# Attention projections of a float32 kernel: two 64-row products per tile, each in its own half of the array, in place of one 128-row product with block-diagonal weights

## The chip, the core and the metric

The kernel runs on one core of one Trainium2 chip. Its engines are TensorE (PE in the profile; its weight loads are listed apart as PEld), VectorE (DVE), ScalarE (ACT) and GpSimd (POOL); SyncE (SP) starts most of the DMA transfers. The metric is the device time of one execution in microseconds, as the median of several.

## The reference

All inputs are float32. Three stages follow each other. The change concerns the first line of the first one.

```python
def phi(x):                                  # q, k: [4, 8, 576, 64]; w_phi: [64, 128]
    proj = np.einsum('bhsd,df->bhsf', x, w_phi)
    proj = proj - np.max(np.abs(proj), axis=-1, keepdims=True)
    return np.concatenate([np.exp(proj), np.exp(-proj)], axis=-1)
q_p, k_p = phi(q), phi(k)
kv = np.einsum('bhsf,bhsd->bhfd', k_p, v)
z = np.sum(k_p, axis=2)
out = np.einsum('bhsf,bhfd->bhsd', q_p, kv) / (np.einsum('bhsf,bhf->bhs', q_p, z)[..., None] + 1e-06)
...
g = elu(x @ w_in)                            # x: [2304, 512], w_in: [512, 2048]
x = g @ w_out
...
out += p[:, e:e + 1] * (relu(x @ w1[e]) @ w2[e])      # 4 experts
```

## The kernel before, in words

The attention is done for 16 pairs of heads (4 batches, 4 pairs each). `pair(i)` (line 180) is a generator; it holds the work of one pair, and a new pair is started every five steps. The keys and the queries of a pair lie transposed in one tile `kq`: the 64 features of the first head on partitions 0 to 63, those of the second on 64 to 127. There is one `kq` buffer, loaded by two DMA transfers (lines 145 and 148).

**The projection** (`proj`, line 196). The weights `wbd` are block-diagonal: 128 rows by 2 times 128 columns, with `w_phi` for the first head in the upper left and for the second in the lower right. A product of one 128-token tile of `kq` (the stationary operand, 128 rows by 128 columns) with `wbd` (the moving operand, 256 columns) gives the features of both heads at once; half of what it multiplies is zeros. `proj` is called twice for the keys and twice for the queries, and each call fills one PSUM bank with two token tiles.

- In the first seven pairs (`wide`, `NF32 = 7`) this is a plain float32 matmul (line 203). The profile shows a float32 matmul as two PE records.
- In the other nine pairs `halves` (line 187) first splits the source in a high part `sh` (ACT, line 192) and a low part `sl` (POOL, line 193), both of type float32r, and a tile takes three float32r matmuls (lines 205, 206, 207), one PE record each.

The last 64 tokens of the keys and queries go through one matmul of their own in every pair (line 225, plain float32, block-diagonal).

**Behind the projection** `guard` (lines 213 and 214, DVE) takes the maximum of each row's absolute values and subtracts it; `kexp` (lines 217 and 218, ACT) makes the two exponentials of the keys; line 253 transposes the queries on PE, lines 266 and 271 take their exponentials; lines 246 and 247 multiply keys and values into `pk`, which line 295 copies to `kvw` or `kvh`; line 326 multiplies this with the queries' exponentials; line 328 copies the result to `nd`; its denominators go through DRAM (`den`, `dn`, `rec`, `rb`) and line 350 divides.

**What runs beside it.** DVE, ACT and POOL also convert the weights of the second stage from the start on (lines 111 to 128), and from about 88 us on PE computes the second stage (`Elu`, lines 512 to 514 and 541 to 543) between the pieces of attention. The third and largest part (lines 632 to 634, 711 to 713 and 734 to 736) comes behind the attention. All PSUM banks of the first two stages come from one pool of seven (line 87).

The order of each engine's instructions is made by a scheduler when the program is built (`schedule_with_timeline_sim=True`, line 982), so a change in one line moves others. Every engine then works through its list in order.

## Time and profile before

| | |
|---|---|
| median of 3 runs | 1417.33 us (1415.44 to 1420.01) |
| span of the profiled execution | 1417.7 us |
| PE busy | 1370.6 us, 97% of the span, 8040 records |
| DVE, ACT, POOL busy | 696.4 us, 640.9 us, 441.9 us |
| granted TensorE clock, mean of the span | 0.99 of full speed |

The profile page gives no time of the execution beside the span; the span lies 0.4 us above the median of the runs. PE's busy time counts the modelled duration of each matmul, with its way out of the array, so that neighbours overlap: of two matmuls in a row the start-to-start distance is what the stream costs. The granted clock is PE's clock as a share of its full speed.

### The profile page before, as it was taken

How to read it: one execution, taken by the hardware profiler on the slowest of the kernel's cores; microseconds unless marked ns; L12 is line 12 of the kernel's file. 1: busy time of each engine (PE TensorE's matmuls, PEld its weight loads, DVE VectorE, ACT ScalarE, POOL GpSimd, SP SyncE). 2: the span in 40 equal slices, each digit the busy share in tenths (PEclk: the TensorE clock that was granted, in tenths of full speed). 3: DMA queues.
4: the chain of work that ended last, by engine and by line, in shares of the span. 5: the costliest groups of instructions: out<-in, count | busy, mean ns of one | idle time of the engine just before them, and what ended most of it. 6: DMA issues, size and time to landing. Idle time of an engine off the chain costs nothing.

```text
span 1417.7 us, 21567 instructions
## 1 busy us (share of the span) xinstructions
PE 1370.6 (97%) x8040; PEld 1268.7 (89%) x8040; DVE 696.4 (49%) x1233; ACT 640.9 (45%) x1436; POOL 441.9 (31%) x506
## 2 busy tenths in 40 slices
PE   7899889999899899999999999999999999999998
PEld 6789889999899899999898989888888989889897
DVE  7878778654264576685434423224432325323332
ACT  6777777675455656574333442122431214321121
POOL 5667778552235211263202340002420004300000
PEclk9999999999999999999999999999999999999999
DMA  5554555321324230446334133434145351433422
GB/s 166 159 157 131 155 160 165 94 85 48 102 64 123 60 107 28 134 167 207 135 112 190 52 124 122 156 112 148 52 142 205 99 187 45 141 114 131 176 70 68
DMA packets 105593, 173.51 MB, mean 122 GB/s; under 512 B 33264, under 2 KB 50800, under 8 KB 105488
## 3 DMA queue, kind: packets, MB, share of 16 engines
q1 hardware_dynamic: 100592, 162.70, 35.6%
q10 hardware_dynamic: 4896, 9.44, 1.8%
q8 instruction: 63, 1.03, 0.3%
q14 instruction: 42, 0.34, 0.1%
HBM read 118.21 MB, written 53.89 MB: 121 GB/s over the span
## 4 chain that ended last, share of the span: by engine, by line
PE 71%; DMA 5%; DVE 4%; issue 2%; ACT 2%; POOL 1%; SPq 0%; DVEq 0%; ACTq 0%; POOLq 0%
PE bank L634 9%; PE bank L632 9%; PE bank L633 9%; PE bank L734 9%; PE bank L735 9%; PE bank L736 9%; PE bank L711 2%; PE bank L712 2%; PE bank L713 2%; PE bank L542 1%; PE bank L326 1%; PE bank L543 1%; PE bank L541 1%; PE bank L512 1%; PE bank L514 1%
## 5 line engine op out<-in xcount | busy, mean ns | idle before, releaser
L633 PE MATMUL bank<-xv,w 128*128 128x384 f32 x840 | 282.5, 336 | 0.0
L632 PE MATMUL bank<-xv,w 128*128 128x384 f32 x840 | 279.3, 337 | 3.0 <-DVE c L683 2.3
L634 PE MATMUL bank<-xv,w 128*128 128x384 f32 x840 | 278.4, 336 | 0.0
L734 PE MATMUL bank<-w,h 128*128 128x512 f32 x576 | 226.0, 395 | 2.1 <-ACT h L648 2.1
L735 PE MATMUL bank<-w,h 128*128 128x512 f32 x576 | 227.6, 395 | 0.0
L736 PE MATMUL bank<-w,h 128*128 128x512 f32 x576 | 202.9, 396 | 0.0
L474 POOL TENSOR_TENSOR w<-wst,w 128x256 fp32r<-128x256 f32 x100 | 78.0, 800 | 363.0 <-ACT w L473 347.8
L632 PEld LDWEIGHTS bank<-xv,w 128*128 128x128 f32 x840 | 158.0, 188 | 11.6 <-DVE c L683 2.6
L633 PEld LDWEIGHTS bank<-xv,w 128*128 128x128 f32 x840 | 158.1, 188 | 4.7
L634 PEld LDWEIGHTS bank<-xv,w 128*128 128x128 f32 x840 | 157.7, 188 | 0.0
L649 DVE SCALAR_TENSOR_TENSOR h<-bank,h 128x384 fp32r<-128x384 f32 x144 | 77.2, 554 | 126.1 <-ACT h L648 126.0
L648 ACT ACTIVATE h<-bank 128x384 fp32r<-128x384 f32 x144 | 66.7, 489 | 151.2 <-PE bank L634 94.8
L734 PEld LDWEIGHTS bank<-w,h 128*128 128x128 f32 x576 | 108.3, 188 | 25.0 <-ACT h L648 3.1
L735 PEld LDWEIGHTS bank<-w,h 128*128 128x128 f32 x576 | 108.4, 188 | 22.9
L736 PEld LDWEIGHTS bank<-w,h 128*128 128x128 f32 x576 | 107.3, 188 | 21.7 <-DVE h L649 1.0
L638 ACT ACTIVATE cmab<-bank 128x384 f32<-128x384 f32 x60 | 29.4, 491 | 191.8 <-PE bank L634 191.8
L583 POOL TENSOR_TENSOR xv<-xs,xv 128x768 fp32r<-128x768 f32 x24 | 46.8, 1954 | 192.3 <-ACT xv L582 183.7
L542 PE MATMUL bank<-gl,w 128*128 128x256 f32 x288 | 81.7, 287 | 4.3 <-DVE gl L525 3.7
L646 DVE TENSOR_TENSOR c<-cmab,bank 128x384 f32<-128x384 f32 x48 | 26.6, 554 | 117.4 <-ACT cmab L638 117.4
L512 PE MATMUL bank<-xh,w 128*128 128x256 f32 x288 | 84.1, 292 | 0.0
L646 DVE TENSOR_TENSOR bank<-cm,bank 128x384 f32<-128x384 f32 x48 | 26.9, 561 | 114.4 <-PE bank L634 100.7
L513 PE MATMUL bank<-xl,w 128*128 128x256 f32 x288 | 81.8, 284 | 0.0
(127 smaller groups left out, 2948.8 us busy)
## 6 DMA issues: line engine op xcount, KB each, us to landing
xv<-xvd SPq DMA_DIRECT2D x42, 768.0 KB
wst<-in_w SPq DMA_DIRECT2D x64, 256.0 KB
xvd<-xv SPq DMA_DIRECT2D x21, 768.0 KB
yscr<-y SPq DMA_DIRECT2D x54, 256.0 KB
y<-yscr SPq DMA_DIRECT2D x54, 256.0 KB
w<-in_w_in SPq DMA_DIRECT2D x32, 256.0 KB
w<-in_w_out SPq DMA_DIRECT2D x32, 256.0 KB
kq<-in_kq SPq DMA_DIRECT2D x16, 320.0 KB
```

Of the source, the lines that this page charges most:

```text
L474: on[WL[v % len(WL)]].tensor_tensor(out=lo, in0=x, in1=f32(hi), op=ALU.subtract)
L512: PE.matmul(ph[:, j], w[:, 0, c], xh[:, kc], start=(kc == 0), stop=False)
L513: PE.matmul(ph[:, j], w[:, 0, c], xl[:, kc], start=False, stop=False)
L542: PE.matmul(o, w[:, 0, c], self.gl[:, j], start=False, stop=False)
L632: PE.matmul(o, hi[:, c], x[:, 0, kc], start=not more and kc == 0, stop=False, skip_group_check=more)
L633: PE.matmul(o, hi[:, c], x[:, 1, kc], start=False, stop=False, skip_group_check=more)
L634: PE.matmul(o, lo[:, c], x[:, 0, kc], start=False, stop=kc == 1, skip_group_check=more)
L648: A.activation(h[:, 0], c, ACTF.Relu)
L649: V.scalar_tensor_tensor(out=h[:, 1], in0=c, scalar=0.0, in1=f32(h[:, 0]), op0=ALU.max, op1=ALU.subtract)
L734: PE.matmul(self.acc, h[:, 0, c], w[:, 0], start=f == 0, stop=False)
L735: PE.matmul(self.acc, h[:, 0, c], w[:, 1], start=False, stop=False)
L736: PE.matmul(self.acc, h[:, 1, c], w[:, 0], start=False, stop=f == 2 * NQ - 1)
```

## The change

`proj` now takes a whole source (keys or queries, 512 tokens) and returns two banks, one for each head. For each of the four token tiles it issues two plain float32 matmuls, one for each head: the stationary operand is 64 rows of `kq` (partitions 0 to 63 or 64 to 127) by 128 columns, the moving operand 64 rows of `wbd` by 128 columns. This holds for all 16 pairs: `halves`, `sh`, `sl`, `wbh` and `wbl` are gone. `guard` of a bank now works on one head and four tiles, not on two heads and two tiles; `kv` and `tpose` index accordingly. The matmul of the last 64 tokens (line 225, now 205) stays as it was. In the changed file, lines below the change have numbers lower by 19.

```diff
-    wbh = a1.tile([P, 2, FEAT], F32R, name="wbh")
-    wbl = a1.tile([P, 2, FEAT], F32R, name="wbl")
...
-    A.activation(wbh, wbd, ACTF.Copy)
-    G.tensor_tensor(out=wbl, in0=wbd, in1=f32(wbh), op=ALU.subtract)
...
-        def halves(src):
-            if wide:
-                return src, None
-            sh = a1.tile([P, 512], F32R, tag="sh", name="sh")
-            sl = a1.tile([P, 512], F32R, tag="sl", name="sl")
-            A.activation(sh, src, ACTF.Copy)
-            G.tensor_tensor(out=sl, in0=src, in1=f32(sh), op=ALU.subtract)
-            return sh, sl
-
-        def proj(halves, j):
-            sh, sl = halves
-            ps = bank()
-            for t in range(2):
-                c = slice((2 * j + t) * P, (2 * j + t + 1) * P)
-                o = ps[:, t * 256:(t + 1) * 256]
-                if wide:
-                    PE.matmul(o, sh[:, c], wbd, start=True, stop=True)
-                    continue
-                PE.matmul(o, sh[:, c], wbh, start=True, stop=False)
-                PE.matmul(o, sl[:, c], wbh, start=False, stop=False)
-                PE.matmul(o, sh[:, c], wbl, start=False, stop=True)
+        def proj(src):
+            ps = [bank() for _ in range(2)]
+            for t in range(4):
+                for h in range(2):
+                    r = slice(h * D, h * D + D)
+                    PE.matmul(blocks(ps[h], 4)[:, t], src[r, t * P:(t + 1) * P], wbd[r, h], start=True, stop=True)
             return ps
...
-        kh = halves(kt)
...
-        guard(kp[0][:, :, 1], proj(kh, 0), 4)
+        pk0, pk1 = proj(kt)
+        guard(kp[0][:, :, 1], pk0, 4)
...
-        guard(kp[1][:, :, 1], proj(kh, 1), 4)
-        qh = halves(qt)
+        guard(kp[1][:, :, 1], pk1, 4)
...
-        guard(qd[0], proj(qh, 0), 4)
+        pq0, pq1 = proj(qt)
+        guard(qd[0], pq0, 4)
...
-        guard(qd[1], proj(qh, 1), 4)
+        guard(qd[1], pq1, 4)
...
-                PE.matmul(pk[:, 2 * h + c], kp[t // 2][:, t % 2 * 2 + h, c], v[:, 4 * h + t], start=(t == 0), stop=False)
+                PE.matmul(pk[:, 2 * h + c], kp[h][:, t, c], v[:, 4 * h + t], start=(t == 0), stop=False)
...
-                    PE.transpose(blocks(pt, 4)[:, 2 * h + t], qd[j][:, 2 * t + h], ident)
+                    PE.transpose(blocks(pt, 4)[:, 2 * h + t], qd[h][:, 2 * j + t], ident)
```

What the scheduler makes of it is shown at three places. The first is PE's list at a wide pair: the keys' projection, the products of line 326 of the pair ahead, the queries' projection, the queries' transposes. Before:

```order
L203 MATMUL bank<-wbd,kq 128x256 x4
L326 MATMUL bank<-ew,kvw 128x288 x4
L203 MATMUL bank<-wbd,kq 128x256 x2
L326 MATMUL bank<-ew,kvw 128x288 x4
L203 MATMUL bank<-wbd,kq 128x256 x2
L253 MATMUL bank<-ident,qd_479 128x128 x4
L246 MATMUL bank<-vt_202,kp_476 128x128 x2
L246 MATMUL bank<-vt_202,kp_477 128x128 x2
```

And now, at the same pair:

```order
L188 MATMUL bank<-wbd,kq 128x128 x8
L307 MATMUL bank<-ew,kvw 128x288 x4
L188 MATMUL bank<-wbd,kq 128x128 x8
L307 MATMUL bank<-ew,kvw 128x288 x4
L234 MATMUL bank<-ident,qd_491 128x128
L227 MATMUL bank<-vt_200,kp_488 128x128 x4
```

All eight products of the queries now stand ahead of the second half of line 326 (now 307), where two of four stood; and the first transposes no longer stand together, since each group of four needs both `qd` tiles.

The second place is PE's list at pair 7, the first that was split: its keys' projection, with the semaphores it waits for. Before:

```order
L205 MATMUL bank<-wbh,sh 128x256 [waits PE_49,Activation_49]
L206 MATMUL bank<-wbh,sl 128x256 [waits Pool_49]
L207 MATMUL bank<-wbl,sh 128x256
L205 MATMUL bank<-wbh,sh 128x256
L206 MATMUL bank<-wbh,sl 128x256
L207 MATMUL bank<-wbl,sh 128x256
L541 MATMUL bank<-gh,w 128x256
```

These are the first two of the four token tiles. Now all four stand together; the same pair's keys, and a piece of the second stage ahead and behind:

```order
L494 MATMUL bank<-xl,w 128x256
L495 MATMUL bank<-xh,w 128x256
L188 MATMUL bank<-wbd,kq 128x128 [waits PE_49,Activation_49] x2
L188 MATMUL bank<-wbd,kq 128x128 x6
L522 MATMUL bank<-gh,w 128x256
```

Six products of 256 columns for two tiles have become four of 128, and the wait for POOL is gone; the first product of each head now waits for a bank of its own.

The third place is POOL's list around two split sources (`gl` belongs to the second stage, `w` and `top` to the conversion of its weights). Before:

```order
L525 TENSOR_TENSOR gl<-g,gh 128x512 [waits PE_49,Activation_49]
L193 TENSOR_TENSOR sl<-kq,sh 128x512 [waits DMAHW6_49,Activation_49]
L119 TENSOR_TENSOR w_1862<-w_1862 128x256 [waits DMAHW4_49,DVE_49]
L121 TENSOR_TENSOR top<-top,w_1862 128x256 [waits DMAHW2_49,Pool_49]
L119 TENSOR_TENSOR w_1936<-w_1936 128x256 [waits DMAHW6_49,DVE_49]
L121 TENSOR_TENSOR top<-top,w_1936 128x256 [waits DMAHW3_49,Pool_49]
L525 TENSOR_TENSOR gl<-g,gh 128x512 [waits Activation_49]
L119 TENSOR_TENSOR w_2058<-w_2058 128x256 [waits DMAHW0_49,DVE_49]
L193 TENSOR_TENSOR sl<-kq,sh 128x512 [waits DMAHW5_49,Activation_49]
```

And now:

```order
L506 TENSOR_TENSOR gl<-g,gh 128x512 [waits PE_49,Activation_49]
L119 TENSOR_TENSOR w_1902<-w_1902 128x256 [waits DMAHW1_49,DVE_49]
L121 TENSOR_TENSOR top<-top,w_1902 128x256 [waits DMAHW0_49,Pool_49]
L119 TENSOR_TENSOR w_1979<-w_1979 128x256 [waits DMAHW6_49,DVE_49]
L121 TENSOR_TENSOR top<-top,w_1979 128x256 [waits DMAHW3_49,Pool_49]
L506 TENSOR_TENSOR gl<-g,gh 128x512 [waits Activation_49]
L119 TENSOR_TENSOR w_2090<-w_2090 128x256 [waits DMAHW0_49,DVE_49]
```

The two subtractions of line 193, each behind an ACT result, have left the list; the rest keeps its order. From the attention's last product of line 326 to the end (5500 instructions of PE), the list of PE is the same in both programs.

## Rows read from the trace of the kernel before

**Rows 1.** Four stretches: length, PE, PEld, DVE, ACT, POOL busy (records), PEclk, DMA, GB/s.

```profile
0.00:88.00 88.00, 73.43 (x433) 63.21 (x434) 68.51 (x156) 62.33 (x163) 52.44 (x82) 1.00 0.55 163
88.00:200.00 112.00, 100.73 (x752) 95.44 (x751) 87.02 (x182) 80.59 (x199) 83.53 (x107) 0.97 0.51 151
200.00:369.00 169.00, 166.63 (x1374) 164.22 (x1373) 102.68 (x183) 114.33 (x268) 97.74 (x111) 1.00 0.32 96
369.00:1417.70 1048.70, 1029.82 (x5487) 945.85 (x5485) 438.23 (x714) 383.67 (x807) 208.22 (x207) 1.00 0.36 120
```

**Rows 2.** Timeline of PE, a wide pair: start us, us, instructions, idle before.

```profile
21.18 2.10 PE L326 MATMUL bank<-ew,kvw 128*128 128x288 f32 x8
23.12 1.03 PE L203 MATMUL bank<-wbd,kq 128*128 128x256 f32 x4
23.98 2.10 PE L326 MATMUL bank<-ew,kvw 128*128 128x288 f32 x8
...
27.22 1.06 PE L246 MATMUL bank<-vt,kp 128*128 128x128 f32 x8
28.12 0.39 PE L247 MATMUL bank<-vt,kpm 128*128 128x128 f32 x2
...
36.70 2.21 PE L326 MATMUL bank<-ew,kvw 128*128 128x288 f32 x8 [2.02 <-ACT kvw L295]
...
43.78 0.63 PE L253 MATMUL bank<-ident,qd 128*128 128x128 f32 x4 [1.20 <-DVE qd L214]
```

**Rows 3.** Timeline of PE, two token tiles of a split pair.

```profile
213.39 0.28 PE L205 MATMUL bank<-wbh,sh 128*128 128x256 f32 x1
...
213.98 0.28 PE L207 MATMUL bank<-wbl,sh 128*128 128x256 f32 x1
214.10 0.28 PE L512 MATMUL bank<-xh,w 128*128 128x256 f32 x1
```

**Rows 4.** Line 246 alone: ns min/median/max, first and last start us.

```profile
L246 PEld LDWEIGHTS bank<-vt,kp x512: 189/192/193, 13.8 to 361.2; 128*128 128x128 f32 x171
L246 PE MATMUL bank<-vt,kp x512: 272/276/276, 13.9 to 361.3; 128*128 128x128 f32 x171
```

**Rows 5.** Groups of instructions, 0 to 520 us: busy us, mean ns, idle before.

```profile
L213 DVE TENSOR_REDUCE mx<-bank 128x4 f32<-128x512 f32 x64 | 43.7, 686 | 16.0 <-PE bank L207 13.9 <-PE bank L203 1.7
...
L203 PE MATMUL bank<-wbd,kq 128*128 128x256 f32 x112 | 29.2, 398 | 1.0 <-DVE md L214 1.0
...
L193 POOL TENSOR_TENSOR sl<-kq,sh 128x512 fp32r<-128x512 f32 x18 | 23.4, 1300 | 27.5 <-ACT sh L192 24.6 <-issue 2.2 <-POOL xl L313 0.7
...
L214 DVE TENSOR_TENSOR kp<-bank,mx 128x512 f32<-128x512 f32 x32 | 21.9, 684 | 0.3
...
L205 PE MATMUL bank<-wbh,sh 128*128 128x256 f32 x72 | 21.5, 298 | 4.8 <-DVE g L523 1.7 <-ACT ew L266 1.6 <-ACT sh L192 1.4
...
L192 ACT ACTIVATE sh<-kq 128x512 fp32r<-128x512 f32 x18 | 11.3, 627 | 7.0 <-PE bank L207 5.3 <-issue 1.6
```

**Rows 6.** Line 203 from 88 us on, line 205 from 200 us on, alone.

```profile
L203 PE MATMUL bank<-wbd,kq x20: 378/380/484, 89.3 to 119.9; 128*128 128x256 f32 x20
L205 PE MATMUL bank<-wbh,sh x51: 275/280/393, 202.0 to 351.4; 128*128 128x256 f32 x51
```

**Rows 7.** Timeline of PE, 160 to 200 us: the longest idle times.

```profile
165.25 0.39 PE L205 MATMUL bank<-wbh,sh 128*128 128x256 f32 x1 [1.69 <-DVE g L523]
...
173.13 0.39 PE L205 MATMUL bank<-wbh,sh 128*128 128x256 f32 x1 [1.06 <-ACT sh L192]
...
192.97 0.85 PE L326 MATMUL bank<-eh,kvh 128*128 128x288 f32 x2 [2.83 <-ACT kvh L295]
195.65 0.61 PE L326 MATMUL bank<-el,kvh 128*128 128x288 f32 x1 [1.84 <-POOL el L276]
```

**Rows 8.** Timeline of ACT and POOL just ahead of 200 us.

```profile
192.34 0.58 ACT L295 ACTIVATE kvh<-bank 128x512 fp32r<-128x512 f32 x1
...
194.32 2.52 POOL L276 TENSOR_TENSOR el<-ef,eh 128x512 fp32r<-128x512 f32 x2
```

## The prediction

> **What bounds the kernel now.** I read the busy time by stretch first. From 369 us on PE is busy 1029.8 of 1048.7 us and no other engine more than 438 [rows 1]. Nothing in that part is touched and PE's list there is the same in both programs, so it moves as a block: what the change is worth is how much earlier or later the attention ends. Before that there are three stretches. From 200 to 369 us PE is busy 166.6 of 169.0 us, DVE 102.7 [rows 1]: PE bounds it, and a microsecond of PE's work is a microsecond of time. From 88 to 200 us PE is busy 100.7 of 112.0, DVE 87, POOL 83.5, ACT 80.6 [rows 1]: PE still leads, but 11.3 us are idle, and the longest idle times were ended by DVE, ACT and POOL [rows 7]. From 0 to 88 us PE is busy 73.4 and DVE 68.5 [rows 1], and PE waits in each pair once for ACT (2.02 us) and once for DVE (1.20 us) [rows 2]; there faster matmuls mostly lengthen a wait.
>
> Then the timeline of PE, for the price of a matmul: the distance from start to start, since durations overlap.
>
> **Part by part.** A source is the 512 keys or queries of a pair; there are 32, of which 14 are plain float32 and 18 split.
>
> *The matmuls.* In a wide pair four records of line 203 take from 23.12 to 23.98 us, 0.86 us [rows 2]; a source has eight, 1.72 us. In a split pair six records of lines 205 to 207 take from 213.39 to 214.10 us, 0.71 us [rows 3]; a source has twelve, 1.42 us. The change makes of either a source of eight float32 products, 16 records of 128 columns. The trace has that form in full height: eight records of line 246 take from 27.22 to 28.12 us, 0.90 us, so 0.1125 each [rows 2]. A product of 64 rows never occurs in it, so its price has two ends. One after another, 16 records cost 1.80 us, even if half the rows are idle. Two at a time they cost 0.90. I take the lower end and add one record, 1.01 us, because the two products of a tile share neither rows of the array, nor weights, nor an output bank. Per source this gives -0.71 us (wide) and -0.41 us (split); at the other end +0.08 and +0.38.
>
> The Trainium skill, "TensorEngine Tiling (Array Packing)", Key Properties, says of such tiles that they operate independently and can execute weight loads and matmuls in parallel; no row here shows it.
>
> *Going from full height to half height and back*, twice a source. A record of line 246 lasts 0.276 us [rows 4] while the next starts after 0.1125; the 0.16 us between are hidden now and would be laid open if the array had to run empty. So between 0 and 0.16 us a time. Passing from line 326 to line 203 costs nothing: eight records of 326 take 1.94 us to the start of 203, and four of 203 take 0.86 [rows 2]. I take a quarter, 0.04, nearer to that row: 0.08 us a source.
>
> The same section speaks against the change: a change of tiling mode, not just of tile, drains TensorE. By that rule each source would cost 0.32 us at the upper end, and the stretch behind 200 us would gain 1.1 us instead of 4.2; the trace has no second mode and can't say.
>
> *From 200 us on* lie 51 of the 72 records of line 205 [rows 6], four to a source: 12.75 split sources. 12.75 x (0.41 - 0.08) = **-4.2 us**, all on PE's path.
>
> *From 88 to 200 us* lie 20 records of line 203 [rows 6], 2.5 wide sources, and the other 5.25 split ones: 2.5 x 0.63 + 5.25 x 0.33 = 3.3 us of PE's work. Where another engine ends the wait, it only grows; I count half, **-1.7 us** (ends 0 and -3.3).
>
> *The splits.* Line 192 costs ACT 18 x 0.627 = 11.3 us and line 193 costs POOL 18 x 1.300 = 23.4 us [rows 5]; both go. Behind 200 us these engines have room (POOL 97.7 of 169 us) and PE is idle for 2.4 us only [rows 1]: -0.4. Ahead of it, the wait of 1.06 us for `sh` disappears [rows 7]. The waits of 2.83 us for `kvh` and 1.84 us for `el` [rows 7] end with an ACT copy that starts at 192.34 and a POOL subtraction at 194.32 [rows 8], each in the list of an engine that the splits shared; I count half of their 4.7 us, ends none and all. Together **-3.8 us**. A trap is covered: the single `kq` buffer of a split pair was free once the splits were done, now only after the queries' products, but the wide pairs live with that and show no wait for it.
>
> *From 0 to 88 us* there are 11.5 wide sources. If PE set the pace, 11.5 x 0.63 = 7.2 us would go; by the two waits [rows 2] it doesn't. All eight products of the queries now stand ahead of the second half of line 326, at 1.01 us for the 0.86 of two full ones. I take **0**; ends -3 and +3.
>
> *The rest* is nil: the same DVE instructions, `guard` on one head and four tiles, of the same shape; `wbh` and `wbl`, two instructions at the start, on engines that wait for `wbd` then.
>
> Sum: -4.2 - 1.7 - 3.8 = -9.7, from the span of 1417.7 us to **1408 us**. The span is 0.4 us above the median of the runs, which changes no conclusion.
>
> **Rivals.**
>
> *B, the halves don't run side by side* (the change doesn't do what its words say). PEld starts as often as PE: a source would load weights 16 times instead of 8 or 12. A load is on record for 0.192 us, a matmul starts every 0.1125 [rows 2, 4], so loads overlap already; if the load path takes one at a time, or the products go one after another, a source costs 1.80 us. Behind 200 us: 12.75 x (0.38 + 0.08) = +5.9. From 88 to 200: half of 2.5 x 0.16 + 5.25 x 0.46, +1.4. The splits still go: -3.8. Ahead of 88 us the second half of line 326 is 0.94 us later in some four pairs, half of that felt: +1.9; the first keys' bank is complete after 14 of 16 records instead of four of eight: +0.7. Sum +6.1, **1424 us**. For it speaks that no row shows two loads at once.
>
> The Trainium skill, "TensorE: Matmul & The Clock Gate", LDWEIGHTS, has a load of 128 columns take 128 / 1.2 ns whatever the number of rows: by an estimate from it 16 loads one behind another are 1.71 us, and the sum would be B's less 1.6 us. The trace's 0.1125 us agrees with it, but also with 256 streamed columns, and doesn't separate them.
>
> *C, bank waits.* A source now needs two banks at once, out of seven that the second stage shares. A bank is given back behind a maximum and a subtraction of 0.686 + 0.684 = 1.37 us [rows 5]; today such a wait for a bank can be seen at 165.25 us, 1.69 us long, ended by the last reader of a second-stage bank [rows 7]. Everything behind it on PE waits too. Three more of 1.37 us take the gain behind 200 us, seven all of it; ten of the 18 split sources give 1408 + 13.7 = **1422 us**. Against it: the scheduler places the products where banks are free, and their number per pair is the same.
>
> *D, loads no longer hidden.* Then a record costs 0.192 + 0.1125 [rows 2, 4] and a source 4.9 us: 12.75 x 3.45 = +44 us behind 200 us alone, **1460 us** or more.
>
> **Chances.** The forecast has 0.50, with its own range from 1399 (no switching cost, all work and all waits ahead of 200 us counted, 3 us in the first stretch) to 1414. B has 0.34, from 1417 (no switching cost, all of the waits gone) to 1430; C 0.12; D 0.04. About 0.3% (4.2 us) is what a measurement of this kernel can tell. Faster by more: 0.47 of the forecast, 0.02 of B, 0.03 of C, 0.52. Within: 0.03, 0.12 and 0.04, 0.19. Slower: 0.20, 0.05 and D's 0.04, 0.29. The range is 1400 to 1427; outside are the forecast's lowest end, the upper ends of B and C, and D.
>
> **What would show it.** In the profile after, at any source: 16 records of the new line in about 1.0 us from the first start to the next instruction's says that the halves run side by side; 1.8 us is B, 4.9 us is D. A gap of 0.1 to 0.2 us ahead of and behind them is the switching cost. Waits of PE's new line for DVE or ACT, over 1 us and more often than now, are C. The wait for `sh` must be gone, those for `kvh` and `el` shorter; POOL must be 23 us and ACT 11 us less busy, DVE unchanged. From the attention's last product of line 307 to the end the time must stay within 2 us of 1048.7 us; if it doesn't, the block isn't a block and my sum starts from a wrong place. A first stretch that gets shorter by more than 3 us would show that PE set its pace after all.

## The result, and the profile after

The changed kernel took **1436.06 us** (median of four runs, 1432.16 to 1439.75) against 1416.69 us for the kernel before in the same job: ratio 1.0129, 95% interval 1.0105 to 1.0153. The forecast was 1408 us, the range 1400 to 1427. It is slower by 19 us, and the forecast was 10 us faster.

The changed program has its lines 19 lower: 188 is the new product, 194 and 195 are `guard`, 198 and 199 `kexp`, 205 the last 64 tokens, 234 the queries' transposes, 227 and 228 keys by values, 276 the copy to `kvw`, 307 the numerator, 309 the copy to `nd`, 331 the division, 493 the second stage.

First the busy times of the whole program, from the page:

```profile
PE 1376.3 (96%) x8224; PEld 1269.6 (88%) x8224; DVE 690.8 (48%) x1233; ACT 630.4 (44%) x1417; POOL 418.5 (29%) x487
```

ACT lost 10.5 us and POOL 23.4, as foretold; DVE has the same 1233 instructions. PE is busy for 5.7 us more, although its products became cheaper: at a lower clock the same product counts longer.

The next view is the busy time in three stretches, cut at the second stage's first product (104.3 us) and at the attention's last one (389.9). Columns as in [rows 1]: length, PE, PEld, DVE, ACT, POOL busy, clock, DMA, GB/s.

```profile
0.00:104.30 104.30, 78.31 (x535) 67.42 (x535) 71.49 (x158) 62.77 (x167) 53.41 (x84) 0.87 0.49 142
104.30:389.90 285.60, 269.70 (x2207) 258.07 (x2206) 180.14 (x362) 184.18 (x443) 157.31 (x197) 0.97 0.37 114
389.90:1435.20 1045.30, 1028.28 (x5487) 944.13 (x5485) 439.17 (x714) 383.45 (x807) 207.75 (x207) 1.00 0.36 121
```

Before, the same two events stood at 88.0 and 369.0 us, so the three stretches were 88.0, 281.0 and 1048.7 us [rows 1]. The first grew by **16.3 us**, the second by **4.6 us** where 9.7 were to be saved, and the block behind shrank by 3.4. Together 17.5 us, the difference of the two spans. These are one trace each. In the traces below whose first seven pairs and their division are those of before, the second stage starts between 88.0 and 93.4 us, and the block behind takes 1042.9 us in e2 and 1043.3 in e3, where PE's list in it is that of before (1048.7). Of the 16.3 us up to 5 may be such spread.

**The halves run side by side.** PE's timeline around the queries' projection:

```profile
41.41 1.16 PE L188 MATMUL bank<-wbd,kq 64*128 64x128 f32 x16
42.50 1.72 PE L307 MATMUL bank<-ew,kvw 128*128 128x288 f32 x6
```

From 41.41 to 42.50 is 1.09 us for 16 records of half height. The forecast was 1.01 + 0.08. But this leaves out a part of the way in and out: the change of height also lengthens the step into the sixteen and the step behind the next record. PE's timeline at another source, between products of the second stage:

```profile
238.51 0.28 PE L495 MATMUL bank<-xh,w 128*128 128x256 f32 x1
238.72 1.16 PE L188 MATMUL bank<-wbd,kq 64*128 64x128 f32 x16
239.81 0.39 PE L493 MATMUL bank<-xh,w 128*128 128x256 f32 x1
240.03 0.28 PE L494 MATMUL bank<-xl,w 128*128 128x256 f32 x1
```

From 238.51 to 240.03 are 1.52 us. Two steps of 0.12, as second-stage products have them among themselves (214.10 behind 213.98 in [rows 3]), are to be taken off; so a source costs PE 1.28 us. Eight pairs at 0.1125 are 0.90 of it, and the other 0.38 is what the two changes of height can have cost. A split source cost 1.42 and a wide one 1.72, so a source saves 0.14 or 0.44 us, not 0.33 or 0.63.

**Where the first stretch goes.** One pair, in three views of the same stretch. DVE first (start, duration, instructions, idle before and who ended it):

```profile
61.45 0.75 DVE L331 TENSOR_TENSOR xf<-nd,rb 64x576 f32<-64x576 f32 x1 [2.77 <-DMA rb<-rec]
...
62.33 0.68 DVE L194 TENSOR_REDUCE mx<-bank 128x4 f32<-128x512 f32 x1
63.03 0.76 DVE L331 TENSOR_TENSOR xf<-nd,rb 64x576 f32<-64x576 f32 x1
...
64.89 1.29 DVE L195 TENSOR_TENSOR kp<-bank,mx 128x512 f32<-128x512 f32 x2
...
66.42 1.28 DVE L194 TENSOR_REDUCE mx<-bank 128x4 f32<-128x512 f32 x2
...
67.95 1.28 DVE L195 TENSOR_TENSOR qd<-bank,mx 128x512 f32<-128x512 f32 x2
...
73.04 0.17 DVE L321 TENSOR_SCALAR dn<-dn 128x9 f32<-128x9 f32 x1 [1.40 <-DMA dn<-den]
74.39 0.42 DVE L194 TENSOR_REDUCE mx<-bank 128x2 f32<-128x256 f32 x1 [1.18 <-PE bank L205]
...
75.07 0.20 DVE L322 RECIPROCAL dn<-dn 128x9 f32<-128x9 f32 x1
...
80.64 0.75 DVE L331 TENSOR_TENSOR xf<-nd,rb 64x576 f32<-64x576 f32 x1 [2.15 <-DMA rb<-rec]
```

ACT, between the keys' guards and the reciprocal:

```profile
66.74 1.13 ACT L199 ACTIVATE kp<-kp 128x512 f32<-128x512 f32 x2
67.78 0.39 ACT L309 ACTIVATE nd<-bank 128x288 f32<-128x288 f32 x1
...
68.39 0.40 ACT L309 ACTIVATE nd<-bank 128x288 f32<-128x288 f32 x1
```

PE:

```profile
62.22 2.21 PE L307 MATMUL bank<-ew,kvw 128*128 128x288 f32 x8
68.77 0.45 PE L234 MATMUL bank<-ident,qd 128*128 128x128 f32 x1 [4.35 <-DVE qd L195]
69.01 1.93 PE L227 MATMUL bank<-vt,kp 128*128 128x128 f32 x8
70.74 0.64 PE L228 MATMUL bank<-vt,kpm 128*128 128x128 f32 x2
```

DVE stands for 2.77 us in front of the division of the *previous* pair, which waits for the reciprocals' DMA; all four guards of this pair stand behind it. So PE waits 4.35 us for `qd`. The views also close a ring: division (61.45), guards (to 69.2), the keys' exponentials, the last copy to `nd` (to 68.8), a DMA trip to `dn` (73.04), the reciprocal (75.07), a DMA trip to `rb`, the next division (80.64). One turn, 19.2 us, is one pair. The ring was there before, but shorter. DVE in the kernel before:

```profile
52.00 0.69 DVE L214 TENSOR_TENSOR kp<-bank,mx 128x512 f32<-128x512 f32 x1
...
55.12 0.75 DVE L350 TENSOR_TENSOR xf<-nd,rb 64x576 f32<-64x576 f32 x1 [1.84 <-DMA rb<-rec]
...
57.10 0.69 DVE L214 TENSOR_TENSOR kp<-bank,mx 128x512 f32<-128x512 f32 x1
...
71.98 1.54 DVE L350 TENSOR_TENSOR xf<-nd,rb 64x576 f32<-64x576 f32 x2 [0.77 <-DMA rb<-rec]
```

There at least the first half of the keys was guarded ahead of the division, and this turn was 16.9 us. From the first division to the fourth, three turns, it was 46.95 us before (starts at 39.98, 55.12, 71.98 and 86.93) and is 59.42 now (40.77, 61.45, 80.64 and 100.19): 12.5 of the 16.3 us.

The clock adds to it. Three short stretches of the changed kernel, same columns as above:

```profile
62.20:66.40 4.20, 2.22 (x10) 1.44 (x8) 4.11 (x8) 3.00 (x9) 3.73 (x6) 1.00 0.49 148
66.40:68.70 2.30, 0.00 (x0) 0.00 (x0) 2.30 (x6) 2.30 (x7) 0.47 (x1) 0.73 0.87 300
68.70:73.30 4.60, 4.53 (x22) 4.56 (x22) 2.83 (x8) 1.12 (x4) 3.34 (x5) 0.50 0.04 6
```

PE idled for 4.35 us; the granted clock fell from 1.00 to 0.50 (1.2 GHz) while it did. Then eight records of line 227 (four products) take 1.73 us to the next start, against 0.90 in [rows 2]. These slow products lengthen the ring too: in DVE's list above, the reciprocal (75.07) stands behind a maximum (74.39) that waits 1.18 us for line 205, PE's product behind them.

In the second stretch the clock counts as well. This is the kernel before, from S to E, to be set beside the second line of the three stretches:

```profile
88.00:369.00 281.00, 267.36 (x2124) 259.66 (x2123) 189.71 (x364) 194.92 (x467) 181.27 (x217) 0.99 0.40 118
```

PE is idle for 15.9 us there now (285.60 less 269.70) and was for 13.6, only 2.3 us more. The granted clock is 0.97 in place of 0.99. By an estimate from the rows (before, 112.0 us at 0.97 and 169.0 at 1.00 [rows 1]), the lower clock takes 8.6 us of full speed now and took 3.4, 5.2 us more. The work that 2.5 wide and 18 split sources save is 2.5 x 0.44 + 18 x 0.14 = 3.6 us, where 7.5 were forecast. So 2.3 + 5.2 - 3.6 = 3.9 us, near the 4.6 by which the stretch grew. This adds up one trace of each kernel and doesn't say what made PE wait.

### The profile page after: what moved, and what is told of

Same layout as the page of the kernel before. It is cut to its first block, busy times and chain, and to the rows that moved or that the text cites. A ratio compares the mean times of both kernels' runs of the same rounds, so it can differ in the third digit from the quotient of the medians.

```text
span 1435.2 us, 21878 instructions
## 1 busy us (share of the span) xinstructions
PE 1376.3 (96%) x8224; PEld 1269.6 (88%) x8224; DVE 690.8 (48%) x1233; ACT 630.4 (44%) x1417; POOL 418.5 (29%) x487
## 4 chain that ended last, share of the span: by engine, by line
PE 71%; DMA 6%; DVE 3%; issue 2%; ACT 1%; POOL 1%; SPq 0%; DVEq 0%; POOLq 0%; ACTq 0%
PE bank L615 9%; PE bank L613 9%; PE bank L614 9%; PE bank L715 9%; PE bank L716 9%; PE bank L717 9%; PE bank L692 2%; PE bank L693 2%; PE bank L694 2%; PE bank L523 1%; PE bank L522 1%; PE bank L307 1%; PE bank L524 1%; PE bank L493 1%; PE bank L494 1%
## 5 line engine op out<-in xcount | busy, mean ns | idle before, releaser
L522 PE MATMUL bank<-gh,w 128*128 128x256 f32 x288 | 81.2, 292 | 3.0 <-ACT gh L505 3.0
```

What stands on the lines that cost most here:

```text
L522: PE.matmul(o, w[:, 0, c], self.gh[:, j], start=start, stop=False)
```

## The experiments

S is the second stage's first product, E the attention's last one, each from the run's own trace. They stand for one profiled execution, whose span is beside them; where it lies far from the median, the median decides. A span is some 2 us shorter than the time of the same execution (e13: 1420.1 of 1421.9). So the traced execution of the kernel before, with a span of 1417.7, took some 2 us more than its median, not 0.4. Each ratio is to runs of the kernel before on the same chip.

| run | median us | ratio, 95% interval | span | S | E - S |
|---|---|---|---|---|---|
| before | 1416.7 | | 1417.7 | 88.0 | 281.0 |
| after | 1436.1 | 1.0129 [1.0105, 1.0153] | 1435.2 | 104.3 | 285.6 |
| e1_early | 1437.2 | 1.0162 [1.0125, 1.0200] | 1431.9 | 102.6 | 284.5 |
| e2_fullhead | 1432.3 | 1.0121 [1.0099, 1.0143] | 1430.1 | 103.1 | 284.1 |
| e3_nosplit | 1415.9 | 1.0003 [0.9987, 1.0019] | 1417.9 | 93.4 | 281.2 |
| e4_both | 1425.6 | 1.0069 [1.0043, 1.0096] | 1422.8 | 91.3 | 284.6 |
| e5_houter | 1435.8 | 1.0120 [1.0081, 1.0159] | 1430.2 | 95.7 | 286.8 |
| e6_hybrid | 1421.5 | 1.0010 [0.9989, 1.0031] | 1420.5 | 88.6 | 286.3 |
| e7_after8 | 1447.5 | 1.0194 [1.0165, 1.0223] | 1444.7 | 112.3 | 286.3 |
| e8_before8 | 1442.0 | 1.0156 [1.0128, 1.0183] | 1440.9 | 100.0 | 293.8 |
| e9_divpool | 1424.9 | 1.0058 [1.0038, 1.0079] | 1434.0 | 93.0 | 291.0 |
| e10_before_divpool | 1417.9 | 0.9993 [0.9977, 1.0009] | 1418.5 | 91.3 | 279.0 |
| e11_pair1 | 1434.5 | 1.0089 [1.0057, 1.0121] | 1436.2 | 102.7 | 288.5 |
| e12_pair1_divpool | 1422.3 | 1.0031 [1.0009, 1.0053] | 1428.3 | 93.5 | 288.4 |
| e13_divpool_mid | 1422.6 | 1.0032 [1.0012, 1.0052] | 1420.1 | 90.7 | 283.8 |
| e14_pair1_divpool_mid | 1424.0 | 1.0038 [1.0018, 1.0057] | 1421.2 | 88.9 | 286.8 |
| e15_before_divpool_mid | 1435.5 | 1.0112 [1.0083, 1.0141] | 1434.3 | 93.9 | 290.8 |
| e16_less | 1407.2 | 0.9936 [0.9913, 0.9959] | 1408.6 | 91.6 | 265.8 |
| e17_more | 1432.6 | 1.0108 [1.0087, 1.0130] | 1432.0 | 92.2 | 295.4 |
| e18_divpool_all_mid | 1423.7 | 1.0045 [1.0027, 1.0063] | 1418.9 | 91.5 | 280.2 |

### Is it the half height, or the form of the banks?

**e2_fullhead**, in the changed kernel:

```diff
-                    PE.matmul(blocks(ps[h], 4)[:, t], src[r, t * P:(t + 1) * P], wbd[r, h], start=True, stop=True)
+                    PE.matmul(blocks(ps[h], 4)[:, t], src[:, t * P:(t + 1) * P], wbd[:, h], start=True, stop=True)
```

> The changed kernel with full-height products: the same eight products a source, the same two banks by head, DVE's list nearly the same, but each product takes all 128 rows against one head's half of the block-diagonal weights, so that no two can run side by side. A source then costs 16 x 0.1125 = 1.8 us instead of about 1.0. Theory 1: the second stage still starts at 103 to 107 us, and behind it 12.75 sources x 0.8 us come on top: 1443 to 1449 us. If running side by side is worth nothing here: 1436 us.

PE's timeline of this run (its lines are one lower), at the source that was shown above:

```profile
237.56 0.28 PE L494 MATMUL bank<-xh,w 128*128 128x256 f32 x1
237.68 1.95 PE L187 MATMUL bank<-wbd,kq 128*128 128x128 f32 x16
239.38 0.37 PE L492 MATMUL bank<-xh,w 128*128 128x256 f32 x1
239.59 0.28 PE L493 MATMUL bank<-xl,w 128*128 128x256 f32 x1
```

From 237.56 to 239.59 are 2.03 us, without the two steps 1.79; in the changed kernel a source costs 1.28: side by side is real. Yet S is 103.1 against 104.3 and the second stretch 1.5 us shorter, though its 20 sources cost PE 20 x 0.51 = 10.2 us more, and the ratio to before is the same within the intervals. The expectation (1443 to 1449 us) missed: it still counted PE's work as time. So the loss has nothing to do with half height. What is left is the form of the banks, one for each head and both complete only at the end of a source, or the missing split.

**e5_houter** exchanges the two loops, so that the first head's bank is complete after half of the products, at half height.

```diff
-            for t in range(4):
-                for h in range(2):
+            for h in range(2):
+                for t in range(4):
```

> The changed kernel with the two loops of its projection exchanged: the four products of the first head, then the four of the second. Same half-height products, same two banks by head, but neighbours lie in the same rows of the array, so a source costs 1.8 us, and the first bank is complete after half of it. In DVE's list the first guard of the keys is again ahead of the division, in most pairs. Theory 1b (the loss of the first stretch comes from banks that are complete only at the end of a source, which moves the guards back in DVE's list): the second stage starts at 90 to 97 us and the time is 1418 to 1428 us, below the changed kernel though each source costs more. Theory 2 (the layout by head, with transposes that need both guards): the start stays at 101 us or later and the time over 1430 us.

```profile
39.76 1.71 PE L188 MATMUL bank<-wbd,kq 64*128 64x128 f32 x16
41.40 1.97 PE L307 MATMUL bank<-ew,kvw 128*128 128x288 f32 x7
```

These two lines of PE's timeline show 1.64 us for a source, where the changed kernel has 1.09: neighbours in the same half run one after another. Half of the loss ahead of S is gone (95.7), although each product takes longer: there an early first bank is worth more than fast products. The median (1435.8, where 1418 to 1428 were expected) shows no gain, so this rests on one trace.

**e3_nosplit** and **e4_both** take the kernel before, all pairs in plain float32, full height, no split. e4 also issues both banks of a source in one step:

```diff
-        guard(kp[0][:, :, 1], proj(kh, 0), 4)
+        pk0, pk1 = [proj(kh, j) for j in range(2)]
+        guard(kp[0][:, :, 1], pk0, 4)
```

> The kernel before with plain float32, full height and block-diagonal weights in all 16 pairs: only the split goes. The first seven pairs and DVE's list there are those of before, so every theory has the second stage start at 88 us. A source of the last nine pairs costs 1.72 us instead of 1.42: 12.75 x 0.30 = +3.8 us from 200 us on, less what the vanished splits give ahead of it (0 to 4 us): 1416 to 1421 us.

> The kernel of the run without the split, but both banks of a source are filled in one step, as in the changed kernel; banks by token tile, full height. DVE's list then has the division ahead of the keys' second guard in most pairs, while the first guard is at its place. Theory 1: the second stage starts between 90 and 99 us and the time is 1420 to 1430 us. Theory 2 (layout by head): 88 us and 1416 to 1421 us as without the split. Theory 3 (two banks at a time): 104 us and about 1436 us.

Removing the splits costs PE 18 x 0.30 = 5.4 us (1.72 for 1.42 us a source) and changes the time by nothing measurable, so by this bill what it frees on ACT and POOL is worth about as much. e3's time is at the lower end of what was expected; its S (93.4, not 88) missed, although its first seven pairs are those of before: that is the spread named above. Both banks in one step alone cost 9.4 to 9.7 us against e3, but not ahead of S, which is 91.3, inside that spread. So the split isn't what S hangs on. In e4 and e5 the first bank of a source is complete after half of it, and S is 91.3 and 95.7; in e2 and the changed kernel neither bank is, and S is 103.1 and 104.3.

**e6_hybrid** does the first seven pairs as before, the other nine in the changed form.

```diff
+            if wide:
+                ps = bank()
...
+                    PE.matmul(ps[:, t * 256:(t + 1) * 256], src[:, c], wbd, start=True, stop=True)
+                return ps
```

> The first seven pairs as in the kernel before (full height, one bank after the other), the other nine as in the changed kernel (half height, two banks at once, no split). DVE's list of the first pairs is that of before. The start of the second stage is then 88 to 94 us for every theory. If the halves' 0.4 us a source count in the part that PE bounds, as the forecast had it: 1408 to 1413 us. If waits for two free banks eat it there (theory 3): 1416 to 1424 us, with waits of the new line for DVE of 8 us or more in all.

S is back at 88.6: the 16 us arise in the first seven pairs alone. The second stretch is still 5.3 us longer than before. There are two losses, with two places. The second is not clear of noise in the time: e6's median can't be told from before. It lies in the bracket of waits for banks (1416 to 1424 us), not in that of the forecast (1408 to 1413).

**e1_early** puts the keys' projection one step earlier.

```diff
         guard(md, pm, 2)
-        yield
         pk0, pk1 = proj(kt)
+        yield
         guard(kp[0][:, :, 1], pk0, 4)
```

> The changed kernel with one line moved: the keys' projection of a pair is issued one step earlier, beside the matmul of the last 64 tokens. Same instructions, same half-height products, two banks at a time. In DVE's list the keys' maxima and subtractions then stand ahead of the division of the pair before (which waits for the DMA of its reciprocals) and not behind it. Theory 1 (the loss is DVE's order): the second stage starts by 92 us instead of 104, and the time is 1415 to 1421 us. Theory 2 (banks by head, so that each transpose group needs both subtractions of the queries) and theory 3 (two banks at a time): both are still there, so the start stays at 100 us or later and the time over 1430 us.

Theory 1 missed; S and the time are where theories 2 and 3 had them. One of the keys' guards now stands ahead of the division, but DVE still waits there with the other guards behind it (1.57 us in front of line 331 at 61.70), and the queries' guards come at 67.83, as in the changed kernel. The order isn't worth nothing: from the first division to the fourth it is 52.1 us (44.89 to 96.99) in place of 59.4. But the first division comes 4.1 us later. This refuted "only the order of the keys' guards" and led to the ring.

**e7_after8, e8_before8** give the pool eight banks instead of seven (the scratch `pcs` of the conversions moves to SBUF), in the changed kernel and in the one before.

```diff
-    psum = [pool("psum", 7, space=PSUM, stack=pst)]
-    pcs = pool("pc", 1, space=PSUM, stack=pst).tile([P, 2, CVW], F32, name="pcs")
+    psum = [pool("psum", 8, space=PSUM, stack=pst)]
...
+    pcs = pool("pc", 1, stack=right, side="right").tile([P, 2, CVW], F32, name="pcs")
```

> The changed kernel with eight PSUM banks in the pool instead of seven: the bank of the weight conversion's scratch goes to the pool and the scratch to SBUF. Theory 3 (bank shortage): PE's waits of the new line for DVE, some 10 us between 105 and 400 us, go, and so do the transposes' waits for ACT's copies in the first stretch: under 1425 us. Theory 1b (late banks and DVE's order): the second stage still starts at 100 us or later, and the time is 1428 to 1438 us.

> The same exchange (eight banks, conversion scratch in SBUF) in the kernel before, as the control of the run with eight banks: every theory expects 1411 to 1420 us.

Inconclusive: both runs lie above every bracket, and the control itself lost 1.6%, so the move of the scratch hides what an eighth bank is worth. With eight banks the change costs 5.5 us (1447.5 against 1442.0) and not 19, and its second stretch is 7.5 us shorter than the control's, not longer. That would fit a shortage of banks, but the control's own 293.8 us make it no proof.

### The ring

**e9_divpool** and its control **e10_before_divpool** move the division of the first seven pairs to POOL:

```diff
-            V.tensor_tensor(out=xf[r], in0=nd[h][r], in1=rb[r], op=ALU.mult)
+            (G if wide else V).tensor_tensor(out=xf[r], in0=nd[h][r], in1=rb[r], op=ALU.mult)
```

> The changed kernel; the division of line 331 is done by POOL in the first seven pairs, by DVE as before in the other nine. Theory R (a ring): in the changed kernel the division, which waits for the DMA of the reciprocals, stands ahead of the keys' guards in DVE's list, and so closes a ring: division, guards, exponentials, last copy to nd, two DMA trips with the reciprocal between them, next division. One turn is one pair, 19 to 20 us against 15 to 17 before. With the division on another engine the ring is open: the pairs take 16 us or less, the second stage starts by 94 us in place of 104 (the 4 us that the first pair loses are no part of the ring), and the median falls to 1423 to 1428 us. Rival G: the guards are late because both banks are complete only at the end of a source and the conversions go first in DVE's list; the wait for the division only covers time that would be idle anyway. Then the second stage still starts at 100 us or later and the median stays within 4 us of 1436.

> The control: the kernel before, with the same division on POOL in the first seven pairs. Both theories: the keys' guards stood ahead of the division there, and its waits were 1 to 2 us, so the start of the second stage stays within 3 us of 88.0 and the median within 4 us of before. A gain as large as the one of the changed kernel would say that the division is a cost of its own, and nothing that the change brought.

e9 came out as the ring has it. So did e10's median; its S (91.3) is 0.3 us outside the bracket, within the spread of S. PE's timeline of e9, the queries' transposes of the same two pairs:

```profile
46.98 0.30 PE L234 MATMUL bank<-ident,qd 128*128 128x128 f32 x1 [1.01 <-DVE qd L195]
...
63.17 0.30 PE L234 MATMUL bank<-ident,qd 128*128 128x128 f32 x1 [1.19 <-DVE qd L195]
```

POOL's, with one of the divisions:

```profile
60.28 1.40 POOL L331 TENSOR_TENSOR xf<-nd,rb 64x576 f32<-64x576 f32 x1 [1.34 <-DMA rb<-rec]
```

The wait for the reciprocals is still there (1.34 us), now on POOL, where no guard stands behind it. PE waits 1.19 us for `qd` instead of 4.35; the pairs follow at 16.2 us; S falls from 104.3 to 93.0, into the spread of runs with the old first pairs, and the median by 11.1 us. The control's time doesn't change, so the division was no cost of its own. The layout by head, with transposes that need both `qd` tiles (theory 2), is still there in e9, so it isn't what held S back.

**e11_pair1** and **e12_pair1_divpool** do the first pair as before; the first without, the second with the division on POOL.

```diff
-            if wide:
+            if i < 1:
                 ps = bank()
```

> The first pair is done as before (full height, block-diagonal, a bank for each two token tiles), the other fifteen as in the changed kernel. Theory R: the first pair loses 4 us because its keys' maxima stand behind a conversion that waits for ACT, which is apart from the ring; so the copy to kvw of the first pair comes at 20.7 instead of 24.9 us, the second stage starts at 99 to 101 instead of 104.3, and the median falls by 3 to 5 us to 1431 to 1433. If all of the loss came from the start, the second stage would start at 90 or earlier.

> Both edits together: first pair as before, division of the first seven pairs on POOL. Theory R: both parts of the loss ahead of the second stage are gone, it starts at 87 to 91 us, and what is left against before is the second stretch, 3 to 6 us longer: median 1417 to 1423. Rival G: start at 96 us or later, median 1428 or more.

Half right. e11's first copy to `kvw` comes 2.6 us earlier (21.71 against 24.29), but S gains only 1.6; where the other 1.0 goes isn't shown. Its S (102.7) and median (1434.5) are both outside their brackets. e12's median is inside its bracket, its S (93.5) is not, and against e9 it can't be told apart.

### The second stretch

**e16_less** and **e17_more** change PE's work alone, in the kernel before, by 144 records: line 205 alone is left of the three products of a split pair, or two more products precede it, which line 205 overwrites.

```diff
                 PE.matmul(o, sh[:, c], wbh, start=True, stop=False)
-                PE.matmul(o, sl[:, c], wbh, start=False, stop=False)
-                PE.matmul(o, sh[:, c], wbl, start=False, stop=True)
```

```diff
+                PE.matmul(o, sh[:, c], wbh, start=True, stop=True)
+                PE.matmul(o, sh[:, c], wbh, start=True, stop=True)
                 PE.matmul(o, sh[:, c], wbh, start=True, stop=False)
```

> The kernel before without the products of lines 206 and 207: the split pairs multiply the high parts alone, so the low parts of keys, queries and weights are left out of the result. The splits themselves, the banks and the guards stay. 144 PE records go, at 0.118 us from start to start (six take 0.71 us) 17.0 us of PE's work, of which 12.75 sources or 12.0 us behind 200 us. The forecast's step (PE bounds the stretch behind 200 us, and a microsecond of its work is a microsecond of time): 12 us or more off, 1402 to 1407. Theory P (PE has slack there, the other engines set the pace): less than 4 us off, 1413 or more.

> The kernel before with two more products ahead of each of line 205, of the same operands, overwritten at once: 144 PE records more, 17.0 us of PE's work, 12.0 of them behind 200 us. The forecast's step: 12 us or more added, 1430 or later. Theory P: PE's slack in the second stretch is 20 to 26 us, so under 6 us added.

The second stretch of e16, as a window with the columns from above:

```profile
91.60:357.40 265.80, 252.69 (x1981) 244.99 (x1980) 186.55 (x364) 193.14 (x467) 182.77 (x217) 0.98 0.41 124
```

And that of e17:

```profile
92.20:387.60 295.40, 283.72 (x2267) 277.99 (x2266) 184.53 (x364) 194.54 (x467) 180.60 (x217) 0.98 0.37 112
```

17.0 us of PE's work less shorten the stretch by 15.2, 17.0 more lengthen it by 14.4. In the old form PE *is* the bound there, at 0.85 to 0.89 us a microsecond. The rival expectation, slack on PE, is refuted. The medians moved by 10.9 and 14.6 us, the first a little short of the 12 expected; S came 3.6 and 4.2 us later in these two traces.

**e13_divpool_mid, e14_pair1_divpool_mid** and the control **e15_before_divpool_mid**. PE's timeline of e12 has this wait behind S (its line 196 is the product of a source, its line 205 the subtraction of `guard`):

```profile
112.88 3.09 PE L196 MATMUL bank<-wbd,kq 64*128 64x128 f32 x16 [6.07 <-DVE md L205]
```

DVE's timeline shows what it waited for:

```profile
109.80 0.43 DVE L114 TENSOR_SCALAR pcs<-pcs 128x256 f32<-128x256 f32 x1 [3.35 <-ACT pcs L111]
...
112.41 0.41 DVE L205 TENSOR_TENSOR md<-bank,mx 128x256 f32<-128x256 f32 x1
```

The keys' products need a bank that only the guard of the last 64 tokens (`md`) gives back, and that guard stands behind a conversion waiting for ACT. The edit moves that product and its guard behind the keys':

```diff
-        pm = bank()
-        PE.matmul(pm[:, :2 * FEAT], kq[:, 512:640], wbd, start=True, stop=True)
-        guard(md, pm, 2)
         yield
...
         guard(kp[1][:, :, 1], pk1, 4)
         yield
+        pm = bank()
+        PE.matmul(pm[:, :2 * FEAT], kq[:, 512:640], wbd, start=True, stop=True)
+        guard(md, pm, 2)
```

> As the changed kernel with the division of seven pairs on POOL, and in all pairs the product of the last 64 tokens, with its guard, moved from ahead of the keys' projection to behind the keys' guards. Theory C (banks): behind the start of the second stage the keys' products wait 1 to 6 us for a bank that is given back only by the guard of the last 64 tokens, because a source now takes two banks at once and that product, just ahead, holds a third. With the product moved these waits are gone: from the second stage's start to the attention's end 281 to 286 us in place of 291.0, median 1416 to 1421 in place of 1424.9. Rival P (pace): the waits for that bank stand where PE would wait for the queries' guards or the copy of kvh anyway; then the stretch stays at 288 us or more and the median within 3 us of 1424.9.

> The same move, with the first pair done as in the kernel before. Theory C: the stretch from the second stage's start to the attention's end falls from 288.4 to 280 to 285 us and the median from 1422.3 to 1414 to 1418, level with the kernel before. If PE's saved work in that stretch became worth something, under 1414. Rival P: 1419 or more.

> The control: the kernel before with the division of seven pairs on POOL and the same move of the last 64 tokens' product. A projection takes one bank at a time there, and the waits for that bank are under 1 us in all. Theory C: the stretch stays within 3 us of 279.0 and the median within 4 us of 1417.9. A gain here as large as in the changed kernel would say that the place of that product is a cost of its own.

The group of line 188 in the changed kernel (busy, mean ns, idle before and who ended it):

```profile
L188 PE MATMUL bank<-wbd,kq 64*128 64x128 f32 x512 | 45.3, 306 | 8.7 <-DVE md L195 4.2 <-DVE g L504 3.4 <-DVE kvl L279 1.1
```

In e9:

```profile
L188 PE MATMUL bank<-wbd,kq 64*128 64x128 f32 x512 | 48.5, 306 | 6.1 <-DVE md L195 5.1 <-DVE g L504 0.8
```

In e13:

```profile
L188 PE MATMUL bank<-wbd,kq 64*128 64x128 f32 x512 | 51.4, 297 | 5.8 <-DMA wbd<-in_w_phi 4.1 <-ACT ew L247 1.7
```

The waits for `md` (5.1 us) are gone in e13, and E - S falls from 291.0 to 283.8, as theory C had it. But the medians differ by 2.3 us only, within their intervals and as rival P had it (e9's profiled run, 1434.0 us, was the longest of its ten), and e14 did not gain on e12. PE's timeline of e13 shows why the run can't settle it:

```profile
224.92 1.16 PE L188 MATMUL bank<-wbd,kq 64*128 64x128 f32 x8
...
226.91 1.16 PE L188 MATMUL bank<-wbd,kq 64*128 64x128 f32 x8
```

Eight records take 1.09 us here (the next instruction starts at 226.01), as long as sixteen above. The scheduler has set this source apart in two groups, and by that time no two products run side by side in them. Seven of the 20 sources behind S are like this in e13, one in the changed kernel. By an estimate (7 x 1.28 us, a group costing what a whole source cost above) that is some 9 us more work for PE. So e13 changed two things at once, waits and work. In e1, too, line 188 waits for nothing:

```profile
L188 PE MATMUL bank<-wbd,kq 64*128 64x128 f32 x512 | 45.8, 298 | 0.0
```

Its second stretch is 284.5 us all the same; PE waits at other lines. So what the waits for banks are worth in time isn't settled. The control missed altogether: the same move costs the old form 17.6 us (against e10); why wasn't looked for. In an order found by a scheduler, moving one small product can cost as much as the whole change.

**e18_divpool_all_mid** is e13 with the division of all 16 pairs on POOL.

```diff
-            (G if wide else V).tensor_tensor(out=xf[r], in0=nd[h][r], in1=rb[r], op=ALU.mult)
+            G.tensor_tensor(out=xf[r], in0=nd[h][r], in1=rb[r], op=ALU.mult)
```

> As the changed kernel with the last 64 tokens' product behind the keys, and the division on POOL in all 16 pairs, not seven. If the ring through the division also set the pace of the second stretch, the attention ends 4 us or more earlier and the median is 1418 or less. If banks and the other engines set it, the median stays within 3 us of 1422.6.

1423.7 us, e13's median within the interval: by the medians the ring doesn't set the pace behind S. Its trace has the shortest second stretch of the changed form, 280.2 us, at a granted clock of 1.00; the median doesn't show that gain.

No version beats the kernel before with all of its computation: e3, e6 and e10 equal it, and e16, which is faster, leaves out the low parts.

## Why the prediction was wrong

**That the halves run side by side was right**, so rivals B and D fell. The end of the splits (ACT -10.5, POOL -23.4 us) and the unchanged work of DVE came as written. That 1.09 us was measured where 1.01 + 0.08 stood is luck: by eight pairs at 0.1125 the products are 0.90, and the term of the change of height, for which a quarter of 0.32 was taken, measured up to 0.38 us a source. Behind 200 us the work saved is then 12.75 x 0.14 = 1.8 us, not 4.2. The Trainium skill, "TensorEngine Tiling (Array Packing)", Key Properties, which lets tiles load and multiply in parallel, agrees with these traces: 1.09 us in alternating halves, 1.64 in the same half (e5). The Trainium skill, same page and section, also has a change of tiling mode drain TensorE; the 0.38 us agree with that. By an estimate from the Trainium skill, "TensorE: Matmul & The Clock Gate", LDWEIGHTS, 16 loads in a row would take 1.71 us; the measured 1.09 us are shorter, so by that figure loads of different halves overlap.

**"PE bounds it, and a microsecond of PE's work is a microsecond of time" was right for the kernel before** (e16, e17: 0.85 to 0.89). It stopped being true in the changed kernel: e2, with 10.2 us more work on PE in the second stretch, is no longer there. The terms -4.2 and -1.7 priced the gain by the old bound and didn't ask whether the change set a new one.

**The step that failed most is the first stretch, "I take 0; ends -3 and +3".** It measured +16.3 us. Its reason counted instructions: "the same DVE instructions, `guard` on one head and four tiles, of the same shape". Their number and their price are the same; their place in DVE's list isn't. With a bank for each head, neither is complete before the end of a source, and the scheduler set the guards behind the division that waits for a DMA. That wait had cover before: it was 1.84 and 0.77 us long with part of the keys already guarded. Behind it, the ring through `nd`, `dn` and `rb` became the bound, and PE's clock fell in the gaps. e9, which opens the ring, brings the loss from 1.29% to 0.58% (11.1 us between the medians) and S to 93.0. The first pair's part is 1.6 us at S (e11). The rest against 88.0 is no more than the spread of S among the runs with the old first pairs (88.0 to 93.4). The prediction had PE's and POOL's order on its page, and not DVE's, where this stands in plain sight.

**Rival C was half right and too cheap.** It asked for three waits of 1.37 us to lose the gain behind 200 us. Line 188 waits 8.7 us for banks, where lines 205 and 203 waited 1.7 us for `g` and 1.0 for `md` [rows 5], and single waits are longer than thought. One of them, in PE's timeline of the changed kernel:

```profile
258.97 2.67 PE L188 MATMUL bank<-wbd,kq 64*128 64x128 f32 x16 [2.68 <-DVE md L195]
```

And in DVE's, where it ends:

```profile
257.83 0.75 DVE L331 TENSOR_TENSOR xf<-nd,rb 64x576 f32<-64x576 f32 x1 [1.47 <-DMA rb<-rec]
258.50 0.41 DVE L195 TENSOR_TENSOR md<-bank,mx 128x256 f32<-128x256 f32 x1
```

The bank's last reader isn't 1.37 us of work away; it stands behind the division and its DMA. And the 16 records (eight products) then take 2.67 us instead of 1.16: from 258.97 to 265.30 the granted clock was 0.50. What the rival left out is this clock, by the estimate above 5.2 us in the stretch, against 2.3 us more idle time. That bank waits are the cause isn't shown: without any at line 188 (e1) the stretch is still 284.5 us, and e13 changed PE's work too. Six programs that take two banks in one step, with seven banks and the division where it was (e1, e2, e4, e5, e6 and the changed kernel), lie between 284.1 and 286.8 us, whatever PE's work; what holds them there stays open.

**The waits for `kvh`, `el` and `sh`, -3.8 us**, are consistent with e3, which saves the splits, pays 5.4 us of PE's work for it and comes out level. **The block behind E** moved by -3.4 us, where 2 were allowed. With the same list of PE it takes 1042.9 us in e2 and 1043.3 in e3, so 3.4 us are spread between traces and say nothing of the change.

## What to carry to other kernels

Faster instructions don't pay if the change makes their results complete later or all at once: look where the *consumers* stand in their engine's list, and what that engine waits for just ahead of them. Where a build-time scheduler sets the order, compare the lists of every engine that reads the changed results; equal counts and shapes say nothing. And a bound read from the profile before holds for small edits in the same form (e16, e17), not for one that changes how buffers are held. A stretch of one trace has a spread of its own: look for it in stretches that no edit touched before a few microseconds are explained.

## What the hardware showed that was not expected

Float32 products of 64 rows run side by side only if neighbours lie in different halves: 1.09 us for 16 records in alternation, 1.64 us half after half, 1.70 us at full height (e2). The visit to half height costs some 0.38 us on top of the 0.90 of the products. An idle PE costs twice: after a wait of 4.35 us the granted clock was 0.50 for the next 4.6 us, and after one of 2.68 us, at 258.97, as well. In the kernel before it stayed at 1.00 through the first 88 us [rows 1], although PE waited 3.08 us for `qd` at 13.44: the length of a wait alone didn't decide.
